# Moving the turned heads' scores and exponentials into the MLP stage of an attention-plus-MLP block

## The chip, the cores and the metric

The kernel runs on one core of a Trainium2 chip. The metric is the device time of one execution in microseconds (us). Before the change it is 1127.23 us, the median of three runs (1126.95 to 1127.47).

## The reference

The block adds attention and an MLP to its input. Both work on the normalised input; the MLP normalises it once more.

```python
def _A_ref(x, wq, wk, wv, wo):          # one k and v for all 16 heads
    q = (x @ wq).reshape(B, S, H, Dh).transpose(0, 2, 1, 3)
    k, v = x @ wk, x @ wv
    scores = einsum("bhqd,bkd->bhqk", q, k) * Dh ** -0.5
    o = einsum("bhqk,bkd->bhqd", softmax(scores), v)
    return o.transpose(0, 2, 1, 3).reshape(B, S, H * Dh) @ wo

def _B_ref(x, w1, b1, w2, b2):
    h = gelu(layernorm(x) @ w1 + b1)    # the tanh form of GELU
    return h @ w2 + b2

xn = layernorm(x)
return x + _A_ref(xn, ...) + _B_ref(xn, ...)
```

The sizes are S = 2048 tokens, D = 448, H = 16 heads of Dh = 28, F = 1792, all in float32. GELU in its tanh form is h(x) = x (0.5 + 0.5 tanh(0.79788 (x + 0.044715 x^3))).

## The kernel before

The tokens are cut into four row chunks of 512 (CT = 4 tiles of 128). Precision is kept by splitting float32 operands into a high and a low part (names ending in h and l) and adding the products. The order of all instructions is the order in which the Python code issues them: a manual schedule, each engine with its own queue in that order.

**First stage (to about 70 us).** x is loaded, normalised and transposed, q, k and v are projected, and q is stored to DRAM (`qd`). k stays in SBUF as `ks`, v as `vs`. All 16 row tiles of x stay in SBUF (`acc`), since the MLP result is later added to them. The second normalisation of chunk 0 is done here.

**MLP stage (70 to 485 us).** It is a row of 56 slots, 14 pieces of F for each of the four chunks. `slot(n)` issues the first product of piece n (`mlp1`, eleven 512-wide matmuls into the PSUM tile `ph`, of which there is one; the last is L174), then GELU on ACT straight from `ph` (L527), a copy to the high part `hh` (L530), the low part `hl` on POOL (L532), and then the second product of piece n-2 (`mlp2`, twelve 448-wide matmuls into four PSUM tiles `m2`, L541 to L545). Every matmul of these is a yield, and after 20 of each 46 yields (MLP_MAX) the loop issues one step of another job: the maxima. In slots 2, 3, 5, ... 13 of the first chunk the slot begins by splitting a part of w2 (ACT L321, then POOL L322, or DVE for the first one). During a chunk the next chunk is normalised and transposed (`norm_gen`): four times in a chunk four transposes (L254) go through the tile `ph`, issued after the sixth matmul of `mlp2` (`between`). b2 is added to a chunk's rows by POOL (L585).

**The maxima.** Softmax needs the maximum of each row of scores before the exponentials. Each head of each unit takes 16 matmuls of a q tile (`qm`, loaded from `qd`) with `ks` into one of three PSUM tiles `m` (L486), each followed by a DVE maximum (L487). Those that are not done in the MLP stage are done in the attention stage.

**Attention stage (485 to 1118 us).** There are 16 units: four row chunks by four groups of four heads. A unit takes eight steps of two key tiles. A step makes the transposed scores (keys on partitions) of the plain heads in pairs (`scores`, matmuls L795 into one of two PSUM tiles `s`, one exponential of 128x1024 on ACT for a pair, L797) and multiplies the previous step's exponentials with v (`pv`, L726, 16 matmul instructions a step in a block). The maxima enter those scores as two extra rows of the product.

**Turned heads.** In the units of TURNED (2 to 15) the fourth head goes another way. Its scores are made with queries on partitions (`turned_scores`, L746), so that DVE can scale them and find the maximum in one pass (L747, into `raw`), ACT takes the exponential with that maximum as bias (L764), 64 KB DMAs on the SP and POOL queues regroup them in SBUF (L768), and DVE transposes 32x32 blocks (L773). Such a unit has three plain heads: three pairs a step instead of four, and no separate maximum for the fourth head.

The order inside a step is written out in ORDERS, a string for units 0 and 1 each and one for the rest. p is a pair of scores with its exponential, m a maximum, t a turned score, x a turned exponential, T the block transposes, P the block of v products, n and o steps of the normalisation and of the output projection, e the load of the next unit's maxima. Maxima are issued only as far as a quota allows, which grows with `weight` from step to step; where it is used up, the m's that stand later in the string issue nothing. In the last 11 steps (LEAD) the weight is zero. The output projection (`o_jobs`, twelve 448-wide matmuls a row tile) lies in four steps after each chunk.

Of the kernel before, what the change touches and what calls it, by code (L numbers as in the profile page):

```python
# [15 lines left out]
P = 128  # L16
S, D, H, DH, F = 2048, 448, 16, 28, 1792
NT = S // P
CT = 4
# [17 lines left out]
def block_kernel(ctx, tc, x, wq, wk, wv, wo, w1, b1, w2, b2, out):  # L37
# [20 lines left out]
    ad = dram.tile([P, NT, D], F32, name="ad")  # L58
    qd = [dram.tile([D, S], F32, name=f"qd{i}") for i in range(2)]

    acc2 = keep.tile([P, CT, D], F32, name="acc2")
# [5 lines left out]
    acc1 = ph1.enter_context(tc.tile_pool(name="accp", bufs=1)).tile([P, NT - CT, D], F32, name="acc")  # L67

    def acc(t0, n=1):
        tile_, t0 = (acc1, t0) if t0 < NT - CT else (acc2, t0 - NT + CT)  # L70
        return tile_[:, t0:t0 + n, :]

    def row(t):
        return acc(t)[:, 0, :]

# [7 lines left out]
    b1t = wp.tile([P, NF], F32, name="b1t")  # L83
    b2b = wp.tile([P, D], F32, name="b2b")
# [4 lines left out]
    hrp = ph1.enter_context(tc.tile_pool(name="hrp", bufs=3))  # L89

    ph1a = ExitStack()
    wqp = ph1a.enter_context(tc.tile_pool(name="wqp", bufs=1))
    qpp = ph1a.enter_context(tc.tile_pool(name="qpp", bufs=4, space=PSUM))
# [6 lines left out]
    def load_x(t0, n):  # L100
        nc.sync.dma_start(acc(t0, n), xv[:, t0:t0 + n, :])
# [27 lines left out]
    qmt = [qmp.tile([P, CW], F32R, name=f"qm{i}") for i in range(3)]  # L129
    for t in qmt:  # L130
        pool.memset(f(t), 0.0)
# [63 lines left out]
    def bn(t):  # L195
        c = t // CT
        if t % CT == 0:
            sts[c] = tmp.tile([P, CT, 6], F32, name="st", bufs=2)
        dve.bn_stats(sts[c][:, t % CT, :], row(t))
# [20 lines left out]
    def norm_both():  # L220
# [8 lines left out]
        act.activation(warm, one, AF.Gelu_apprx_tanh)  # L229
        yield  # L230

    def norm_parts(c, second, first=False, bank=mtile):
# [5 lines left out]
        def center(k):  # L238
# [6 lines left out]
            act.activation(xn[:, 0:D], row(t), AF.Identity, bias=bias[:, t:t + 1], scale=scale[:, t:t + 1])  # L245
            dve.tensor_scalar(xn[:, D:512], row(t)[:, 384:448], scale[:, t:t + 1], bias[:, t:t + 1],
# [144 lines left out]
    def b1_turn():  # L391
        pb = mtile([P, NF])
        pe.transpose(pb, b1r, ident[0:NF, 0:NF])
        dve.tensor_copy(b1t, pb)

# [8 lines left out]
    def load_m(u, j, qm=None, q=None):  # L404
        c, g = units[u]
        if qm is None:
            qm = qmt[heads.index((u, j)) % 3]
# [8 lines left out]
    for c in range(NCH):  # L416
        center, turn = norm_parts((c + 1) % NCH, c + 1 == NCH)
        for i in range(4):
# [7 lines left out]
            if i in ((2, 3) if c == 0 else (1, 3)):  # L426
# [8 lines left out]
                if n in (2, 3):  # L435
                    qms.append(load_m(*heads[n - 2]))
            for job in more.get((c, i, True), ()):
# [38 lines left out]
    def max_stream():  # L476
        for h, (u, j) in enumerate(heads):
# [3 lines left out]
            for t in range(CT):  # L481
                for n in range(4):
                    if (t, n) == (0, 2) and h + 2 < len(heads):
                        qms.append(load_m(*heads[h + 2]))
# [26 lines left out]

    ph1b = ExitStack()
    hp = ph1b.enter_context(tc.tile_pool(name="hp", bufs=3))
# [7 lines left out]
    def mlp1(c, ft):  # L521
# [4 lines left out]
        hr = hrp.tile([P, CW], F32, name="hr", bufs=2)  # L526
        act.activation(hr, ph, AF.Gelu_apprx_tanh, bias=b1t[:, ft:ft + 1])  # L527
        hh = hrp.tile([P, CW], F32R, name="hh")
        hl = hrp.tile([P, CW], F32R, name="hl")
        act.activation(hh, hr, AF.Copy)  # L530
        hs[c, ft] = (hh, hl)
        pool.tensor_sub(hl, hr, f(hh))  # L532

    def mlp2(c, ft, between):
# [4 lines left out]
        for k in range(CT):  # L539
            ts = slice(k * P, (k + 1) * P)  # L540
            pe.matmul(m2[k], hh[:, ts], w2h[:, ft, :], start=(ft == 0), stop=False)  # L541
            yield
            pe.matmul(m2[k], hh[:, ts], w2l[:, ft, :], start=False, stop=False)  # L543
            yield
            pe.matmul(m2[k], hl[:, ts], w2h[:, ft, :], start=False, stop=(ft == NF - 1))  # L545
            if ft == NF - 1:
                a = row(CT * c + k)
                dve.tensor_add(a, a, m2[k])
                if k == CT - 1 and c < NCH - 1:
                    nc.sync.dma_start(ad[:, CT * c:CT * c + CT, :], acc(CT * c, CT))  # L550
            if k == 1:
                between()
# [329 lines left out]
```

## Time and profile before

| what | value |
|---|---|
| median of three runs | 1127.23 us |
| profiled execution, its own time | 1126.83 us |
| profiled execution, span | 1125.1 us |
| PE busy | 1110.3 us (99%) |
| weight loads (PEld) busy | 713.9 us (63%) |
| DVE busy | 898.1 us (80%) |
| ACT busy | 656.6 us (58%) |
| POOL busy | 474.3 us (42%) |
| DMA moved | 120.05 MB, mean 107 GB/s |

The busy times come from one profiled execution; the engines work side by side. PE is the matrix engine, ACT the activation engine, DVE the vector engine, POOL the general engine, SP the one that only issues DMAs. The durations of matmuls overlap, because they are pipelined, so the distance from one start to the next is what a matmul takes of PE's time. L with a number is a line of the code above. In rows of groups, the numbers behind the bar are busy us and mean ns of one, and behind the second bar the idle time before them with what ended it.

### The profile page before, as it was taken

Reading aid. Unit: us, or ns where it says so; the run is one execution under the profiler, and the core shown is the slowest. Engines: PE = TensorE matmul, PEld = TensorE weight load, DVE = VectorE, ACT = ScalarE, POOL = GpSimd, SP = SyncE. Lnnn points to the kernel's source line nnn. Section 1 sums busy time; section 2 is a strip of 40 time slices with the busy share of each in tenths; the row PEclk is TensorE's granted clock in tenths of the full one; section 3 lists DMA queues with packets and bytes.
Section 4 is the critical chain, followed back from the end, with each engine's and each line's share of the span. In section 5 each row is a group of like instructions: output and inputs, shape, how many; then the busy total and the mean of one; then the engine's idle time right before and its main releaser. Section 6 shows DMA issues by size and latency. Waiting matters only on the chain.

```text
span 1125.1 us, 17754 instructions
## 1 busy us (share of the span) xinstructions
PE 1110.3 (99%) x5793; PEld 713.9 (63%) x5793; DVE 898.1 (80%) x1676; ACT 656.6 (58%) x789; POOL 474.3 (42%) x719
## 2 busy tenths in 40 slices
PE   9999999999999999999999999999999999999998
PEld 8778888888888888854544445544446444455444
DVE  7789999999999999976677877677786777776743
ACT  6752221222222111256888888688886888886883
POOL 6332241113113112311566666366664666653640
PEclk9999999999999999999999999999999999999999
DMA  8661101000100012030455676455665556664520
GB/s 281 198 198 50 58 17 50 25 17 17 58 18 17 25 50 54 22 95 10 117 144 148 168 168 168 136 156 154 158 181 148 155 144 167 164 164 134 139 67 33
DMA packets 73928, 120.05 MB, mean 107 GB/s; under 512 B 24486, under 2 KB 34916, under 8 KB 73836
## 3 DMA queue, kind: packets, MB, share of 16 engines
q1 hardware_dynamic: 53228, 80.26, 25.2%
q0 software_dynamic: 19200, 38.08, 12.7%
q8 instruction: 46, 0.75, 0.3%
q10 hardware_dynamic: 1408, 0.57, 0.2%
q14 instruction: 46, 0.38, 0.1%
HBM read 45.19 MB, written 13.88 MB: 53 GB/s over the span
## 4 chain that ended last, share of the span: by engine, by line
PE 89%; DVE 6%; ACT 2%; issue 2%; DMA 1%; SPq 1%; POOL 0%; DVEq 0%; ACTq 0%; POOLq 0%
PE po L726 20%; PE s L795 18%; PE m L486 16%; PE ph L169 10%; PE m L746 4%; PE m L543 4%; PE m L545 4%; PE m L541 4%; DVE mx L487 3%; PE qp L169 2%; PE m L637 1%; ACT p L797 1%; PE ph L172 1%; PE ph L174 1%; PE m L639 1%
## 5 line engine op out<-in xcount | busy, mean ns | idle before, releaser
L487 DVE TENSOR_REDUCE mx<-m 128x1 f32<-128x512 f32 x800 | 525.9, 687 | 33.4 <-PE m L486 27.9
L797 ACT ACTIVATE p<-s 128x1024 f32<-128x1024 f32 x389 | 381.9, 1024 | 111.2 <-PE s L795 110.4
L486 PE MATMUL m<-ks,qm 128*128 128x512 f32 x800 | 319.9, 405 | 2.1 <-DVE raw L747 1.0
L795 PE MATMUL s<-xh,ks 128*128 128x512 f32 x778 | 261.2, 419 | 3.7 <-ACT p L797 1.8
L768 POOL DMA_DIRECT2D turned<-raw x336 | 168.1, 506 | 213.1 <-ACT raw L764 193.2
L747 DVE TENSOR_SCALAR_CACHE_REDUCE raw<-m 128x512 f32<-128x512 f32 x224 | 151.7, 684 | 119.4 <-PE m L746 95.2
L726 PE MATMUL po<-p,vs 128*32 128x512 f32 x2048 | 247.0, 598 | 0.0
L795 PEld LDWEIGHTS s<-xh,ks 128*128 128x128 f32 x778 | 131.1, 188 | 142.8 <-ACT p L797 109.0
L527 ACT ACTIVATE hr<-ph,b1t 128x512 f32<-128x512 f32 x56 | 38.5, 688 | 305.4 <-PE ph L174 281.6
L532 POOL TENSOR_TENSOR hl<-hr,hh 128x512 fp32r<-128x512 f32 x56 | 72.2, 1290 | 301.5 <-PE m L486 284.4
L486 PEld LDWEIGHTS m<-ks,qm 128*128 128x128 f32 x800 | 150.1, 188 | 54.5 <-DVE raw L747 21.0
L773 DVE STREAM_TRANSPOSE p<-turned 128x1024 f32<-128x1024 f32 x112 | 138.4, 1236 | 22.3 <-PE po L726 8.6
L726 PEld LDWEIGHTS po<-p,vs 128*32 128x32 f32 x2048 | 53.8, 109 | 121.5 <-issue 117.1
L764 ACT ACTIVATE raw<-raw,m 128x1024 f32<-128x1024 f32 x112 | 127.8, 1141 | 0.0
L746 PE MATMUL m<-ks,q 128*128 128x512 f32 x224 | 88.5, 395 | 0.0
L541 PE MATMUL m<-w2h,hh 128*128 128x448 f32 x224 | 82.4, 368 | 0.0
L545 PE MATMUL m<-w2h,hl 128*128 128x448 f32 x224 | 82.0, 366 | 0.0
L543 PE MATMUL m<-w2l,hh 128*128 128x448 f32 x224 | 81.9, 366 | 0.0
L169 PE MATMUL ph<-xh,w1l 128*128 128x512 f32 x168 | 66.2, 394 | 0.0
L169 PE MATMUL ph<-xl,w1h 128*128 128x512 f32 x168 | 66.1, 394 | 0.0
L169 PE MATMUL ph<-xh,w1h 128*128 128x512 f32 x168 | 66.0, 393 | 0.0
L746 PEld LDWEIGHTS m<-ks,q 128*128 128x128 f32 x224 | 42.1, 188 | 10.3 <-DVE raw L747 0.7
(151 smaller groups left out, 1100.1 us busy)
## 6 DMA issues: line engine op xcount, KB each, us to landing
turned<-raw SPq DMA_DIRECT2D x560, 64.0 KB
turned<-raw POOLq DMA_DIRECT2D x336, 64.0 KB, 2.3
xh<-qd POOLq DMA_DIRECT2D x56, 168.0 KB, 4.0
qm<-qd SPq DMA_DIRECT2D x160, 56.0 KB
qd<-qe SPq DMA_DIRECT2D x24, 256.0 KB
tr<-ld POOLq DMA_DIRECT2D x56, 64.0 KB, 2.6
raw<-in_B_w_dram SPq DMA_DIRECT2D x7, 448.0 KB
q<-qd SPq DMA_DIRECT2D x56, 56.0 KB
```

Of the source, the lines that this page charges most:

```text
L169: pe.matmul(ps, w, v, start=(n == 0), stop=False)
L486: pe.matmul(pm, qm[:, t * P:(t + 1) * P], ks[:, n * CW:(n + 1) * CW], start=True, stop=True)
L487: dve.tensor_reduce(mx[:, CT * j + t, n:n + 1], pm, axis=AX.X, op=ALU.max)
L541: pe.matmul(m2[k], hh[:, ts], w2h[:, ft, :], start=(ft == 0), stop=False)
L726: pe.matmul(po[32 * j:32 * j + 32, :], vs[:, kt, :], ps.pop((u, kt, j)), start=(kt == 0), stop=(kt == NT - 1))
L746: pe.matmul(sc, q3[i][:, t * P:(t + 1) * P], ks[:, n * CW:(n + 1) * CW], start=True, stop=True)
L747: dve.tensor_scalar(raw[:, :, 4 * n:4 * n + 4, :].rearrange("p r b i -> p b r i"), sc.rearrange("p (b r i) -> p b r i", r=4, i=32), SCALE, ...
L764: act.activation(raw[:, rs], raw[:, rs], AF.Exp, bias=m3[:, 4:5], scale=1.0)
L768: q.dma_start(turned[u][32 * r:32 * r + 32, 4 * t + a, :], raw[32 * a:32 * a + 32, r].rearrange("p b i -> p (b i)"))
L773: dve.transpose(p.rearrange("p k (g j) -> p g k j", j=32), turned[u][:, :, 32 * kt:32 * kt + 64].rearrange("p g (k j) -> p g k j", j=32))
L795: pe.matmul(s[:, i], ks[:, (kt + k) * P:(kt + k + 1) * P], qss[u][:, j, :], start=True, stop=True)
L797: act.activation(p, s, AF.Exp, scale=SCALE)
```

## The change

- Unit 1 is turned too: TURNED has 15 units.
- The turned heads are scored in the MLP stage. Of the steps that a slot issues beside its matmuls (18 of 46 yields now), the first four are turned scores (`tq.step()`), one row tile of a turned head per slot; the others are maxima. The last turned unit's 16 scores are left for the attention stage.
- The exponentials are taken in the MLP stage too, two of 128x1024 per slot, and stored to DRAM (`td`), four DMAs of 256 KB a row tile on SP. In the attention stage each half of a turned unit is read back by four DMAs of 512 KB, a unit ahead, in the order that the block transposes need. `raw` has two buffers instead of three.
- GELU is worked out from Tanh: Identity (`hx`) and Square (`hz`) read `ph` on ACT; POOL adds one and multiplies; ACT takes Tanh; POOL scales and multiplies; ACT copies the high part and POOL subtracts. The stages are issued at fixed places between the twelve `mlp2` matmuls of the slot: the norm's step after the second (before: the sixth), an exponential after the fourth and the seventh, Tanh after the fifth, the copy after the tenth.
- The rows of x are no longer kept: `line` reloads each row tile in the MLP stage, once for its second normalisation and once for the addition of the MLP result, which is then stored to `ad`. b2 is added row tile by row tile, in slots 11, 12 and 13 of a chunk and 0 of the next. The last chunk's rows are read back at the end like the others.
- The q tiles of the maxima have two buffers instead of three and are loaded one head ahead instead of two.
- ORDERS has one string for unit 0 and one for the others; `weight` is 4 a step in unit 0 and 5 afterwards.

The changed program issues 224 turned scores and 281 of 784 maxima in the MLP stage, and 503 maxima and 16 turned scores in the attention stage. Before, 560 of 800 maxima were in the MLP stage, and 240 maxima and all 224 turned scores in the attention stage.

```diff
-MLP_MAX = 20
-ORDERS = ("ptmpmmpmmenPptmmon", "ptpmmpmxenPptmonm", "ptmpTeonPpxtmn")
-TURNED = tuple(range(2, 16))
-RAWS = 3
+MLP_MAX = 18
+ORDERS = ("pmpmmpmmenPpmmonm", "ptmpmmeTnPpxmmon")
+TURNED = tuple(range(1, 16))
+RAWS = 2
+GELU = 0.044715, 0.7978845608028654
...
+    def line(t):
+        lines[t] = keep.tile([P, D], F32, name="a", bufs=4)
+        nc.sync.dma_start(lines[t], xv[:, t, :])
...
     def turned_exp():
...
         act.activation(raw[:, rs], raw[:, rs], AF.Exp, bias=m3[:, 4:5], scale=1.0)
-        for r in range(2 * h, 2 * h + 2):
-            for a in range(4):
-                q = pool if a == 3 or (a == 2 and r % 2) else nc.sync
-                q.dma_start(turned[u][32 * r:32 * r + 32, 4 * t + a, :],
-                            raw[32 * a:32 * a + 32, r].rearrange("p b i -> p (b i)"))
+        if h == 1:
+            for a in range(4):
+                nc.sync.dma_start(td[u][:, :, 4 * t + a, :],
+                                  raw[32 * a:32 * a + 32].rearrange("p r (h b) i -> p (r h) (b i)", h=2))
+            stored[u] = t
...
     def mlp1(c, ft):
...
-        hr = hrp.tile([P, CW], F32, name="hr", bufs=2)
-        act.activation(hr, ph, AF.Gelu_apprx_tanh, bias=b1t[:, ft:ft + 1])
-        hh = hrp.tile([P, CW], F32R, name="hh")
-        hl = hrp.tile([P, CW], F32R, name="hl")
-        act.activation(hh, hr, AF.Copy)
-        hs[c, ft] = (hh, hl)
-        pool.tensor_sub(hl, hr, f(hh))
+        hx = hrp.tile([P, CW], F32, name="hx", bufs=2)
+        hz = hrp.tile([P, CW], F32, name="hz", bufs=2)
+        act.activation(hx, ph, AF.Identity, bias=b1t[:, ft:ft + 1])
+        act.activation(hz, ph, AF.Square, bias=b1s[:, ft:ft + 1], scale=GELU[0] ** 0.5)
+        pool.tensor_scalar(hz, hz, 1.0, 1.0, op0=ALU.mult, op1=ALU.add)
+        pool.tensor_mul(hz, hz, hx)
+
+        def middle():
+            act.activation(hz, hz, AF.Tanh, scale=GELU[1])
+            pool.tensor_scalar(hz, hz, 0.5, 0.5, op0=ALU.mult, op1=ALU.add)
+            pool.tensor_mul(hx, hx, hz)
+
+        def ending():
+            hh = hrp.tile([P, CW], F32R, name="hh")
+            hl = hrp.tile([P, CW], F32R, name="hl")
+            act.activation(hh, hx, AF.Copy)
+            hs[c, ft] = (hh, hl)
+            pool.tensor_sub(hl, hx, f(hh))
...
     def slot(n):
...
+        stages = {1: norms.get(n, none), 3: turned_exp, 4: middle, 6: turned_exp, 9: ending}
...
+        ts = 0
         for _ in slot(n):
             done += 1
             if n < len(mslots) + 1 and done * MLP_MAX // 46 > (done - 1) * MLP_MAX // 46:
-                maxed += mxs.step()
-        if (c, ft) == (NCH - 1, NF - 1):
-            act.activation(warm, one, AF.Exp)
+                if ts < 4 and n < len(mslots):
+                    ts += tq.step()
+                else:
+                    maxed += mxs.step()
...
+    def load_d(u, h):
+        halves[u, h] = att.tile([P, 4 * CT, 256], F32, name="half", bufs=3)
+        for r in range(4):
+            nc.sync.dma_start(halves[u, h][32 * r:32 * r + 32], td[u][:, 2 * r + h, :, :])
...
-    weight = [0 if n >= len(steps) - LEAD else 24 if n < 6 else 16 if u < 2 else 6 for n, (u, kt) in enumerate(steps)]
+    weight = [0 if n >= len(steps) - LEAD else 4 if u == 0 else 5 for n, (u, kt) in enumerate(steps)]
...
+        if kt % 8 == 0 and u + 1 < NU:
+            load_d(u + 1, kt // 8)
```

More of the change, by code (lines that the diff above doesn't have):

```diff
@@ L394, in b1_turn @@
         dve.tensor_copy(b1t, pb)
+        pool.tensor_scalar(b1s, b1t, GELU[0] ** 0.5, 0.0, op0=ALU.mult, op1=ALU.add)
     later(3, 0, b1_turn)
@@ L546, in mlp2 @@
             if ft == NF - 1:
-                a = row(CT * c + k)
+                t = CT * c + k
+                a = lines.pop(t)
                 dve.tensor_add(a, a, m2[k])
[L549 to L552, printed above, removed]
+                nc.sync.dma_start(ad[:, t, :], a)
+            stages[3 * k + 2]()
             yield
```

157 lines of the change are left out of this document (81 added, 76 removed).

## The prediction

> **What bounds the kernel now.** I read the chain of waits first, then busy time by stage, then the timeline of one MLP slot and of one attention step. The chain that ended last, by engine:
>
> ```profile
> PE 89%; DVE 6%; ACT 2%; issue 2%; DMA 1%; SPq 1%; POOL 0%; DVEq 0%; ACTq 0%; POOLq 0%
> ```
>
> The PE queue sets the time. Stages (start and end, length, then busy us and count of PE, PEld, DVE, ACT, POOL): two pieces of the MLP's first row chunk, from one slot's last projection matmul (L174) to another's; its chunks 2 to 4; attention unit 0; unit 1; the 101 steps with a turned head that still place maxima; one plain MLP slot; one slot with transposes; four attention steps with the output projection.
>
> ```profile
> 69.56:80.01 10.45, 9.66 (x38) 6.71 (x37) 10.32 (x17) 3.48 (x5) 2.59 (x2) 1.00 0.29 73
> 80.01:169.80 89.79, 89.79 (x413) 75.60 (x412) 83.91 (x132) 25.90 (x38) 32.60 (x22) 1.00 0.15 46
> 169.80:475.47 305.67, 305.46 (x1387) 255.86 (x1386) 285.22 (x448) 64.40 (x99) 67.92 (x54) 1.00 0.11 32
> 493.54:536.37 42.83, 41.12 (x215) 20.20 (x214) 28.68 (x54) 28.19 (x34) 5.41 (x5) 1.00 0.20 49
> 536.37:581.42 45.05, 44.57 (x240) 22.35 (x239) 31.11 (x71) 39.54 (x43) 24.72 (x46) 1.00 0.43 123
> 581.42:1067.32 485.90, 483.60 (x2740) 237.06 (x2740) 367.06 (x759) 401.21 (x429) 291.38 (x522) 1.00 0.59 157
> 304.69:311.98 7.29, 7.29 (x34) 6.19 (x33) 7.01 (x13) 1.97 (x3) 1.29 (x1) 1.00 0.12 34
> 319.28:327.13 7.85, 7.85 (x39) 6.50 (x37) 7.52 (x13) 2.57 (x4) 1.29 (x1) 1.00 0.00 1
> 689.77:717.57 27.80, 27.77 (x152) 17.24 (x152) 18.10 (x37) 17.94 (x20) 12.63 (x24) 1.00 0.56 149
> ```
>
> A plain slot is 33 matmuls in 7.29 us (the 34th reaches in), with ACT busy 1.97 and POOL 1.29: reserve on both. In the attention steps ACT is busy 401 of 486 us. The granted clock is 1.00 throughout.
>
> **MLP: what a slot becomes.** PE in a plain slot, starts and durations:
>
> ```profile
> 304.69 0.39 PE L174 MATMUL ph<-xl,w1h 128*128 128x512 f32 x1
> 304.92 0.39 PE L486 MATMUL m<-ks,qm 128*128 128x512 f32 x1
> 305.15 0.36 PE L541 MATMUL m<-w2h,hh 128*128 128x448 f32 x1
> 305.35 0.37 PE L543 MATMUL m<-w2l,hh 128*128 128x448 f32 x1
> ```
>
> Starts lie 0.23 us apart after a 512-wide matmul, 0.20 after a 448-wide one. MLP_MAX 18 instead of 20 gives nine score steps per slot for ten: 7.06 us, over 56 slots **-12.9**.
>
> Four of the nine are turned scores, with two exponentials per slot on ACT, and GELU is now Identity, Square, two POOL operations, Tanh, two POOL operations, Copy, and POOL's subtraction as before. ACT in a slot, then POOL behind it:
>
> ```profile
> 305.18 0.69 ACT L527 ACTIVATE hr<-ph,b1t 128x512 f32<-128x512 f32 x1 [5.94 <-PE ph L174]
> 305.90 0.63 ACT L530 ACTIVATE hh<-hr 128x512 fp32r<-128x512 f32 x1
> 306.44 0.75 ACT L245 ACTIVATE xn<-acc,lnqb,lnq 128x448 f32<-128x448 f32 x1
> ```
> ```profile
> 306.67 1.29 POOL L532 TENSOR_TENSOR hl<-hr,hh 128x512 fp32r<-128x512 f32 x1 [6.00 <-PE m L486]
> ```
>
> ACT follows PE by 0.10 us (304.69+0.39 to 305.18), POOL follows ACT by 0.14 (306.53 to 306.67), and independent activations overlap by 0.09 (306.44). POOL in the attention stage:
>
> ```profile
> 614.98 1.31 POOL L678 TENSOR_TENSOR oc<-oc,tr 128x512 f32<-128x512 f32 x1
> 616.39 0.61 POOL L684 TENSOR_SCALAR oth<-oc 128x512 fp32r<-128x512 f32 x1
> 617.09 1.29 POOL L685 TENSOR_TENSOR otl<-oc,oth 128x512 fp32r<-128x512 f32 x1
> ```
>
> So a multiply takes 1.31, a scalar operation 0.61, with 0.1 between. Square and Tanh are not in the trace; I take 0.69 and 0.64, from L527 and L530. ACT runs its queue in order, so the next slot's Identity stands behind this slot's Copy. The loop: Identity 0.69-0.09, Square 0.69, 0.14, POOL 0.61+0.10+1.31, 0.10, Tanh 0.64, 0.14, POOL 2.02, 0.10, Copy 0.63-0.09 = **6.99 us against a slot of 7.06**. Plain slots stay on PE's pace, but with no reserve: what is put into the loop is paid.
>
> Transposes of the next chunk (12 slots) use the bank `ph`. They moved from after the sixth MLP-2 matmul to after the second, and `ph` is now free only after Square. PE is there 0.23+0.20+0.23+0.20 = 0.86 after L174 starts; Square ends at 0.39+0.10+0.60+0.69 = 1.78. Wait 0.97 with latency, and 0.10 for the slower restart (rows in the attention part): 12 x 1.07 = **+12.9** (0 if the loop were early, 23 if it runs 0.9 late).
>
> ```profile
> L585 POOL TENSOR_TENSOR acc<-acc,b2b 128x448 f32<-128x448 f32 x16 | 17.9, 1152 | 0.0
> L322 POOL TENSOR_TENSOR w2l<-raw,w2h 128x896 fp32r<-128x896 f32 x6 | 12.7, 2122 | 4.3 <-ACT w2h L321 4.1
> ```
>
> The six splits of w2 in chunk 1 stand on POOL ahead of a slot's first GELU operation, which had no room to give: 6 x 2.1 = 12.6. Four slots there are transpose slots of 7.06+(7.85-7.29)+1.07 = 8.7 us, in which the loop (about 7.4 with the norm's ACT work) gains 1.3 each: **+7.4** net (0 to 12.6). The adds of b2 stand in the same place four slots a chunk, mostly drained before the next wait: **+2**.
>
> The first split is worse: ACT's copy of w2h and DVE's subtraction stand at the start of slot 2 behind the Copy of slot 1.
>
> ```profile
> L321 ACT ACTIVATE w2h<-raw 128x896 fp32r<-128x896 f32 x7 | 6.6, 942 | 0.0
> ```
> ```profile
> L322 DVE TENSOR_TENSOR w2l<-raw,w2h 128x896 fp32r<-128x896 f32 x1 | 1.4, 1447 | 0.0
> ```
>
> Two loops after slot 0's L174, 0.49+2x7.0 = 14.5, then 0.94 and 1.45: DVE is held until 16.9, and slot 2's turned scores behind it; with three PSUM banks the fourth waits, and slot 2 ends near 17.9 instead of 10.45: **+7.4** (5 to 8). At the other end hl of the last slot comes 8.7 us after L174 where 7.6 would do: **+2** (0 to 4). MLP together -12.9+12.9+7.4+2+7.4+2 = **+18.8**.
>
> What is queued behind the new waits: the stores of exponentials (60 row tiles, four DMAs each, on SP) wait for the second exponential; behind them stand the loads of q rows (issued 14 maxima ahead, nearly three slots) and of x rows (two slots ahead), so nothing comes late. The tile `raw` has two buffers: its first writer two slots later comes 11.6 us after L174; the second exponential ends near 5.7, the fourth store is issued near 7.5, so it may take 4.2 us.
>
> ```profile
> xh<-qd POOLq DMA_DIRECT2D x56, 168.0 KB, 4.0
> ```
>
> That is the nearest landing (168 KB for 256). It just fits; I cost it at nothing. [...]
>
> **Attention: what a step becomes.** PE in a step, and ACT:
>
> ```profile
> 623.75 0.74 PE L795 MATMUL s<-xh,ks 128*128 128x512 f32 x2
> 624.33 0.40 PE L746 MATMUL m<-ks,q 128*128 128x512 f32 x1
> 624.56 0.63 PE L795 MATMUL s<-xh,ks 128*128 128x512 f32 x2
> 625.03 0.39 PE L746 MATMUL m<-ks,q 128*128 128x512 f32 x1
> 625.26 0.39 PE L486 MATMUL m<-ks,qm 128*128 128x512 f32 x1
> 625.67 0.73 PE L795 MATMUL s<-xh,ks 128*128 128x512 f32 x2
> 626.33 1.92 PE L726 MATMUL po<-p,vs 128*32 128x512 f32 x16
> 628.18 0.73 PE L795 MATMUL s<-xh,ks 128*128 128x512 f32 x2
> ```
> ```profile
> 624.59 1.03 ACT L797 ACTIVATE p<-s 128x1024 f32<-128x1024 f32 x1 [0.62 <-PE s L795]
> ```
> ```profile
> 515.81 0.73 PE L795 MATMUL s<-xh,ks 128*128 128x512 f32 x2 [0.24 <-ACT p L797]
> ```
>
> Three pairs of scores C, A, B share two tiles `s`, so B waits for the exponential of C: 624.59+1.03 = 625.62, and B starts at 625.67, 1.92 after C; in the earlier step that wait is named. (A pair after a pause takes 0.58 to 0.66, one in flow 0.47.) Before, the two or three other matmuls all lie between C and B, where that wait covers them. A step is 1.92 + 0.66 + the po block 1.85 = 4.43.
>
> After, 503 of 784 maxima are left for attention (240 of 800 before): 4.4 a step (503 over 577 units of weight, five a step). The order "ptmpmmeTnPpxmmon" fills them in from its front: one after A, two after B, and what is left, 1.4, after C. C 0.58, 1.4 x 0.23, A 0.47, 0.23: B could start at 1.60 and still waits until 1.92. **The two behind B have no cover: 4.43+0.46 = 4.89.** That ACT lost the 112 exponentials here is no help, for B needs only C's, which ACT begins at once either way.
>
> Per part: the 12 steps with the output projection cost 27.80/4 = 6.95; there its twelve matmuls come to lie between C and A and cover the wait: 0.58+0.3+12x0.2+0.47+0.23+0.47+0.46+0.1+1.85 = 6.86, -1. The other 89 average (485.90-12x6.95)/89 = 4.52, to 4.89: +32.9. Unit 1 drops from four pairs to three, 45.05/8 = 5.63 to 4.89: -5.9. Unit 0 (7 steps, 6.12) takes 3.5 maxima (weight 4): B at 1.92, two maxima, D at 2.96, then 0.66+0.1+1.85 = 5.57: -3.9. The last 11 steps hold no maxima before or after; some turned work ahead goes: -1. **Attention +21** (bounds: 0, if B were early; +40, if also DVE delays the maxima).
>
> ```profile
> L773 DVE STREAM_TRANSPOSE p<-turned 128x1024 f32<-128x1024 f32 x102 | 126.0, 1236 | 6.7 <-DMA turned<-raw 2.9 <-DMA q<-qd 2.0 <-DMA qm<-qd 1.9
> L487 DVE TENSOR_REDUCE mx<-m 128x1 f32<-128x512 f32 x159 | 108.9, 685 | 0.0
> ```
>
> DVE's step is 4.4x0.685+1.24 = 4.25 of 4.89: it keeps up. The read back (512 KB a DMA, eight steps or 39 us ahead) and POOL's DMA issues that go cost and gain nothing; POOL is nowhere on the chain. The table load dropped at the MLP's end lay beside ten us of matmuls: nothing.
>
> **Sum.** The profiled execution took 1126.83 (span 1125.1), 0.4 under the median of 1127.23. 1126.8+18.8+21 = **1167**.
>
> **Rivals.** (1) The ACT-POOL loop is shorter than worked out and PE never waits in the MLP: 1126.8-12.9+21 = 1135. For it: the reserve before; against: the sum of rows is 6.99. (2) B's wait is no floor and the added maxima fill gaps: attention 0, so 1146. PEld is busy 237 of 486 us there, PE 484. [...] The 0.24 us wait on ACT speaks against it: the room is a wait that comes too early in the step to be filled from behind B. (3) Faster: PE is bound by its number of matmuls alone and waits no more than before. 16 fewer (-16 maxima, +16 turned, -16 scores) x 0.23 = -3.7: 1123. It decides if Square frees `ph` before 0.86 us and C's exponential ends within 1.6 us of C; the rows say 1.78 and 1.9. (4) Slower still: the loop outgrows the slot. [...] (5) It doesn't do what it says: its instruction order has the 224 turned scores in the MLP and no table loads between Tanh and Exp, so hardly.
>
> **Chances.** Forecast 0.56 (own range 1152 to 1184), (1) 0.10, (2) 0.10, (3) 0.07, (4) 0.15, no difference 0.02. Range 1135 to 1205: from (1) to the middle of (4). A measurement here can tell about 0.2%: faster 0.07, within it 0.02, slower 0.91.
>
> **What would show it.** Slots 7.06 where plain and 8.5 or more with transposes, PE's idle before them named as ACT's `hz`; slot 2 near 13 us after slot 1; in attention B 1.92 after C, then two maxima, then po, steps of 4.9. Wrong it is if slots run over 7.3 throughout, if `raw`'s writers wait for a DMA, or if steps come near 4.5.

## The result, and the profile after

The changed kernel took 1178.2 us (median of four runs, 1178.14 to 1179.59) beside 1127.3 for the kernel before on the same chip: 1.0455 times as long, interval 1.0437 to 1.0473. The forecast was 1167, its own range 1152 to 1184. The profiled execution has a span of 1177.7 us, 52.6 more than that of before.

The chain of waits by engine, to be held against PE 89% before:

```profile
PE 68%; POOL 11%; ACT 10%; issue 4%; DVE 3%; DMA 2%; SPq 1%; ACTq 0%; POOLq 0%; DVEq 0%
```

POOL and ACT, which held 0% and 2% of the chain, now hold a fifth of it. POOL's part is for the most part GELU's loop; of ACT's 10%, 6% are the exponentials of attention (L830), which held 1% before. Busy time by stage, in the columns of the prediction's table (window, length, busy us and count of PE, PEld, DVE, ACT, POOL, then granted clock, DMA share, GB/s). The rows are: MLP slots 1 and 2; slots 3 to 14; the rest of the MLP; attention unit 0; unit 1; the 101 steps with maxima; a plain slot; a slot with transposes; four steps with the output projection.

```profile
71.27:93.48 22.21, 11.88 (x39) 8.23 (x38) 10.90 (x26) 9.94 (x13) 10.11 (x10) 0.88 0.52 125
93.48:193.75 100.27, 92.58 (x402) 77.03 (x400) 82.04 (x180) 64.60 (x86) 77.16 (x70) 0.94 0.69 176
193.75:501.42 307.67, 296.56 (x1346) 248.02 (x1345) 258.72 (x606) 197.84 (x262) 221.99 (x216) 1.00 0.73 183
521.13:560.74 39.61, 35.73 (x193) 16.30 (x193) 16.38 (x29) 28.18 (x34) 6.06 (x6) 1.00 0.89 195
560.74:600.77 40.03, 39.10 (x217) 18.59 (x216) 34.62 (x55) 25.01 (x28) 14.16 (x23) 1.00 0.41 94
600.77:1121.14 520.37, 506.36 (x2829) 253.51 (x2828) 422.02 (x612) 308.02 (x336) 176.06 (x288) 1.00 0.71 160
298.83:305.86 7.03, 7.03 (x33) 6.01 (x32) 6.06 (x15) 3.98 (x5) 6.08 (x6) 1.00 0.64 161
259.29:267.78 8.49, 7.71 (x38) 6.33 (x37) 7.04 (x18) 5.97 (x9) 6.16 (x6) 1.00 0.76 183
720.03:747.49 27.46, 27.46 (x155) 18.14 (x154) 18.65 (x28) 13.31 (x16) 9.00 (x17) 1.00 0.71 183
```

The MLP, from the first slot's last projection matmul to the last one's, takes 430.15 us for 405.91 (+24.2); attention from the first po block to the last 644.2 for 619.2 (+25). The other 3.4 lie before the MLP (1.7), where PE waits that much for a load of q, and between MLP and attention (1.6). In the 101 steps ACT is busy 308 us for 401: the change did take that work from ACT, and these steps grew by 34.5 all the same. The granted clock (the last column but two) has changed too: it was 1.00 everywhere and is 0.88 and 0.94 in the first two rows.

An attention step, PE and then ACT (three exponentials in one row):

```profile
948.94 0.73 PE L828 MATMUL s<-xh,ks 128*128 128x512 f32 x2
949.52 0.62 PE L491 MATMUL m<-ks,qm 128*128 128x512 f32 x2
949.98 0.62 PE L828 MATMUL s<-xh,ks 128*128 128x512 f32 x2
950.43 0.39 PE L491 MATMUL m<-ks,qm 128*128 128x512 f32 x1
950.86 0.74 PE L828 MATMUL s<-xh,ks 128*128 128x512 f32 x2
951.43 0.63 PE L491 MATMUL m<-ks,qm 128*128 128x512 f32 x2
```
```profile
949.77 2.88 ACT L830 ACTIVATE p<-s 128x1024 f32<-128x1024 f32 x3 [1.97 <-PE s L828]
```

C starts at 948.94, B at 950.86, 1.92 later, with three maxima before it and two behind it, and then the po block at 951.99: the step as forecast. In the MLP, a slot with transposes:

```profile
245.56 0.66 PE L256 MATMUL ph<-ident,xn 128*128 128x128 f32 x4 [0.78 <-ACT hz L572]
```

PE stands for 0.78 us until Square (L572) has read `ph`. Three things were not forecast. In slot 1 ACT waits 8.88 us before it may write `hx`, and PE behind it:

```profile
76.01 0.69 ACT L571 ACTIVATE hx<-ph,b1t 128x512 f32<-128x512 f32 x1 [8.88 <-DMA qd<-qe]
...
77.32 0.50 PE L164 MATMUL ph<-xh,w1h 128*128 128x512 f32 x1 [4.15 <-ACT hz L572]
```

`hx` now lies in memory of the stage before, and waits until the last transfer out of `qe` there has ended. In slot 2 the forecast wait of PE comes, and what follows it is slow:

```profile
92.46 0.80 PE L525 MATMUL m<-ks,q 128*128 128x512 f32 x1 [5.42 <-DVE raw L526]
93.05 0.63 PE L167 MATMUL ph<-xh,w1h 128*128 128x512 f32 x1
93.48 0.63 PE L169 MATMUL ph<-xl,w1h 128*128 128x512 f32 x1
```

Starts of 512-wide matmuls lie 0.43 us apart here and until 98.2, and 0.23 after. And the writers of `raw` wait for the stores of exponentials (us in total, times, longest), three times in chunk 1 (4.1 us), twice in chunk 3 (1.1) and six times in chunk 4 (6.5):

```profile
DVE raw L526 <- DMA td<-raw: 11.7, 11, 2.2
```

### The profile page after: what moved, and what is told of

Same layout as the page of the kernel before. It is cut to its first block, busy times and chain, and to the rows that moved or that the text cites. A ratio compares the mean times of both kernels' runs of the same rounds, so it can differ in the third digit from the quotient of the medians.

```text
span 1177.7 us, 16968 instructions
## 1 busy us (share of the span) xinstructions
PE 1116.2 (95%) x5777; PEld 715.9 (61%) x5777; DVE 914.3 (78%) x1704; ACT 726.4 (62%) x899; POOL 558.3 (47%) x679
## 4 chain that ended last, share of the span: by engine, by line
PE 68%; POOL 11%; ACT 10%; issue 4%; DVE 3%; DMA 2%; SPq 1%; ACTq 0%; POOLq 0%; DVEq 0%
PE po L796 20%; PE s L828 16%; PE m L491 10%; ACT p L830 6%; PE ph L164 5%; POOL hz L574 3%; POOL hx L579 3%; PE m L525 3%; PE m L603 2%; PE m L597 2%; PE m L600 2%; POOL hl L586 2%; PE qp L164 2%; DMA td<-raw 1%; ACT hz L577 1%
## 5 line engine op out<-in xcount | busy, mean ns | idle before, releaser
L492 DVE TENSOR_REDUCE mx<-m 128x1 f32<-128x512 f32 x784 | 511.0, 686 | 115.9 <-PE m L491 107.8
L830 ACT ACTIVATE p<-s 128x1024 f32<-128x1024 f32 x381 | 367.8, 1024 | 234.8 <-PE s L828 234.1
L491 PE MATMUL m<-ks,qm 128*128 128x512 f32 x784 | 287.5, 398 | 1.7 <-DVE mx L492 0.8
L810 DVE STREAM_TRANSPOSE p<-half 128x1024 f32<-128x1024 f32 x120 | 147.8, 1232 | 5.9 <-PE po L796 5.9
L543 ACT ACTIVATE raw<-raw,m 128x1024 f32<-128x1024 f32 x120 | 137.1, 1142 | 0.0
L525 PE MATMUL m<-ks,q 128*128 128x512 f32 x240 | 96.0, 400 | 12.5 <-DVE raw L526 9.1
L586 POOL TENSOR_TENSOR hl<-hx,hh 128x512 fp32r<-128x512 f32 x56 | 72.2, 1290 | 41.6 <-ACT hh L584 40.8
L744 POOL DMA_DIRECT2D tr<-ld x56 | 28.2, 508 | 113.4 <-DMA ld<-rc 113.4
L412 POOL DMA_DIRECT2D qm<-qd x112 | 57.4, 519 | 40.7 <-PE m L491 32.1
L574 POOL TENSOR_TENSOR hz<-hz,hx 128x512 f32<-128x512 f32 x56 | 72.5, 1294 | 4.7
L579 POOL TENSOR_TENSOR hx<-hx,hz 128x512 f32<-128x512 f32 x56 | 72.3, 1291 | 4.7
L577 ACT ACTIVATE hz<-hz 128x512 f32<-128x512 f32 x56 | 35.3, 631 | 61.4 <-POOL hz L574 61.4
L584 ACT ACTIVATE hh<-hx 128x512 fp32r<-128x512 f32 x56 | 35.4, 632 | 60.3 <-POOL hx L579 60.3
```

What stands on the lines that cost most here:

```text
L491: pe.matmul(pm, qm[:, t * P:(t + 1) * P], ks[:, n * CW:(n + 1) * CW], start=True, stop=True)
L492: dve.tensor_reduce(mx[:, CT * j + t, n:n + 1], pm, axis=AX.X, op=ALU.max)
L525: pe.matmul(sc, q3[i][:, t * P:(t + 1) * P], ks[:, n * CW:(n + 1) * CW], start=True, stop=True)
L543: act.activation(raw[:, rs], raw[:, rs], AF.Exp, bias=m3[:, 4:5], scale=1.0)
L574: pool.tensor_mul(hz, hz, hx)
L579: pool.tensor_mul(hx, hx, hz)
```

## The experiments

**The maxima moved from behind B to behind C (x1).** Two of the forecast's steps are at issue: that B waits and that the maxima behind it have no cover.

```diff
-ORDERS = (..., "ptmpmmeTnPpxmmon")
+ORDERS = (..., "ptmmpeTnPpxmmmon")
```

> The changed kernel with one string of ORDERS changed: the maxima of a turned step stand two behind C and two behind A instead of one behind A and two behind B, so that they lie between C and B; nothing else moves. Theory 1 (B may not start before C's exponential ends, 1.92 us after C, and what stands behind B is uncovered): the step goes from 4.89 to C 0.58 + four maxima 0.92 to 1.0 + A 0.47 = 2.0, + 0.66 + 1.85 = 4.55; over 97 steps that is -31 us, so 1147 against 1178. Rival (a step costs what its matmuls cost, wherever the maxima stand): no change, 1178. Rival (DVE sets the step, 4.25 us of work in it): the maxima behind each other wait for DVE and the step stays above 4.75, 1165 or more.

Measured 1171.5, ratio 1.0386 (1.0369 to 1.0403): 6.7 us gained of the 31 expected. Steps without the output projection average 4.80 for 4.92. By the number of maxima in them: in the changed kernel the 43 steps with four and the 25 with five, and no other matmul beside scores and products, all take 4.89, so the fifth costs nothing there; here those with four take 4.49 and those with five 5.10. One with five:

```profile
946.15 0.73 PE L828 MATMUL s<-xh,ks 128*128 128x512 f32 x2
...
947.90 1.10 PE L491 MATMUL m<-ks,qm 128*128 128x512 f32 x2
948.84 0.63 PE L828 MATMUL s<-xh,ks 128*128 128x512 f32 x2
```

B (948.84) now comes 2.69 after C, so it no longer waits for C's exponential; but five maxima stand close, and the last of them waits for one of the three banks that DVE must empty (its start lies 0.60 behind that at 947.90, instead of 0.23; over the run the weight loads of these matmuls wait 48.1 us for DVE's maxima, 3.1 in the changed kernel). So theory 1 holds where four maxima are placed (4.49, for the 4.55 worked out), and with five DVE holds the step longer than the wait had done: the rival named for this run, which gave 1165 or more.

**Half an exponential each (x2).** The exponential of a pair was cut into two, in the same tile, so that B's first matmul could start earlier.

```diff
-        act.activation(p, s, AF.Exp, scale=SCALE)
+            act.activation(p[:, i], s[:, i], AF.Exp, scale=SCALE)   # behind each matmul
```

> The changed kernel with the exponential of a pair of scores taken in two halves of 512 columns, each as soon as its matmul is done; the order of the matmuls is as in the changed kernel. Theory 1: the first half of C is through 0.44 + 0.10 + 0.60 = 1.14 us after C starts, the second near 1.7, so B starts when the queue gets there, 1.6 us after C, instead of 1.92: steps of 4.57 to 4.65 instead of 4.89, -25 to -30 us, 1148 to 1153. Rival (a step costs what its matmuls cost): no change, 1178. Rival (ACT becomes the bound: six halves of 0.60 and 0.04 between are 3.9 us of a step): no loss expected below 4.4 us a step.

Measured 1708 and 1746 us in two runs, far from any expectation. One row of the list of waits (us in total, times, longest), and the attention steps as a window:

```profile
PE s L828 <- ACT p L830: 294.1, 380, 1.7
```
```profile
560.00:1200.00 640.00, 479.66 (x1865) 185.75 (x1865) 283.99 (x418) 256.05 (x441) 119.44 (x192) 0.79 0.37 85
```

The second matmul of a pair waits until the exponential of the first half has read the tile: in this run the order is kept by tile, not by half. So each pair pays matmul, exponential, matmul in turn, and with these waits all through the stage, 0.77 us on average and 1.7 at the longest, the granted clock is 0.79 there, for 1.00 in the changed kernel's steps. The run tells nothing of the floor; x5 makes the same test with separate tiles.

**Square reads `hx` (x3).** It frees `ph` one operation earlier.

```diff
-        act.activation(hz, ph, AF.Square, bias=b1s[:, ft:ft + 1], scale=GELU[0] ** 0.5)
+        act.activation(hz, hx, AF.Square, scale=GELU[0] ** 0.5)
```

> The changed kernel with Square reading hx from SBUF instead of ph, so that ph is free after Identity. Theory 2 (the twelve transpose slots wait for ph until Square ends): the wait of 0.78 us plus restart shrinks by 0.5 to 0.6 in each, -7 us, 1171; transpose slots of the later chunks go from 8.50 to 7.95. Rival (what paces these slots is the loop over ACT and POOL, not ph): Square now starts after Identity ends, the loop grows by 0.1, and nothing is won: 1178 to 1183.

Measured 1178.2 (two runs), ratio 1.045 (1.0429 to 1.047): no change in the whole. In the slots there is one:

```profile
243.68 0.36 PE L600 MATMUL m<-w2l,hh 128*128 128x448 f32 x1
...
244.19 0.33 PE L256 MATMUL ph<-ident,xn 128*128 128x128 f32 x1
```

PE's gap before the transposes is 0.15 us for 0.78, the slots take 8.03 for 8.50, and the MLP 425.3 for 430.2. The profiled run lost those 4.8 elsewhere: 1.8 before the MLP, 1.2 behind it, 1.1 in attention. So the wait for Square is real, and taking it away is worth about half a us a slot; a gain of 3 or 4 us in the total is within what two runs leave open.

**Memory of their own for `hx` and `hz` (x4).** They leave the pool that takes over the first stage's memory; `mr` gets 9 buffers for 14 and `hz` one for two to make room.

```diff
-        hx = hrp.tile([P, CW], F32, name="hx", bufs=2)
+        hx = hxp.tile([P, CW], F32, name="hx", bufs=2)      # pool opened ahead of the first stage
```

> The changed kernel with hx and hz (hz with one buffer) in memory of their own, not in that of the first stage's pool; nothing else moves but the number of buffers of the small maxima tiles. Theory 3 (the 4.2 us stall in slot 1 is Identity of slot 0 waiting for the last store of q, whose memory hx reuses, and the half clock after it is a consequence of the stall): the stall goes, slot 1 takes near 6 instead of 10.98 us, PE's starts stay 0.23 apart there, and of the 4.2 + 1.9 some 4 to 6 us stay won: 1172 to 1174. Rival (the fill of the chain sets the first slots, so the wait only moves to slot 2): 1178, slot 2 longer by what slot 1 loses.

Measured 1175.8, ratio 1.0428 (1.0407 to 1.0449). Slots 1 to 3, in the changed kernel, here, and in x8 (below), each in a row (the second row of x8 is one of its slots with transposes):

```profile
71.27:102.66 31.39, 21.06 (x70) 15.95 (x69) 17.35 (x42) 15.39 (x20) 15.56 (x16) 0.84 0.49 120
```
```profile
72.72:98.72 26.00, 19.57 (x71) 14.55 (x69) 17.03 (x42) 15.17 (x20) 14.46 (x15) 0.87 0.55 135
```
```profile
71.12:93.71 22.59, 19.60 (x70) 14.39 (x69) 15.90 (x40) 14.38 (x19) 14.33 (x14) 0.85 0.54 148
252.37:263.98 11.61, 9.52 (x38) 7.41 (x36) 8.36 (x19) 5.66 (x8) 6.33 (x6) 0.85 0.79 195
```

5.4 us go from these slots, and ACT's wait for `qe` is gone from the list of waits; the MLP takes 424.2. The first of the unforeseen things is shown in the slots; the 2.4 us by which the total is shorter are within what the two intervals leave open.

**Score tiles of one bank (x5).** Four tiles of one bank in place of two of two, with an exponential each.

```diff
-    sp = ctx.enter_context(tc.tile_pool(name="sp", bufs=2, space=PSUM))
+    sp = ctx.enter_context(tc.tile_pool(name="sp", bufs=4, space=PSUM))
...
-        s = sp.tile([P, 2, CW], F32, name="s")
         for i, (k, j) in enumerate(jobs):
-            pe.matmul(s[:, i], ...)
+            s = sp.tile([P, CW], F32, name="s")
+            pe.matmul(s, ...)
+            act.activation(p[:, i], s, AF.Exp, scale=SCALE)
-        act.activation(p, s, AF.Exp, scale=SCALE)
```

> The six score matmuls of an attention step go to four tiles of one bank each instead of two tiles of two banks, and each has its own exponential (0.60 us, six a step, 3.6 us of ACT instead of 3.1). Theory 1 (the step's floor is the wait of the pair B for C's two-bank exponential, 1.92 us after C): a single bank is free about 1.1 us after C starts, so B no longer waits and the step is PE's own work, 1.85 for the po block, 6 x 0.233 for scores, 4.4 x 0.233 for maxima and 0.3 of restarts, about 4.55 instead of 4.89: 105 steps x 0.34 = -36, about 1142 us. Rival (DVE, the three banks of the maxima, paces the steps, as the run with the reordered maxima left 4.76): steps 4.75, about 1162. Rival (the step is bound by its matmuls and not by the wait): 1178.

Measured 1151.9, ratio 1.0222 (1.0205 to 1.0239): 26 us less than the changed kernel.

```profile
860.77 0.74 PE L828 MATMUL s<-xh,ks 128*128 128x512 f32 x2
...
862.28 0.67 PE L828 MATMUL s<-xh,ks 128*128 128x512 f32 x2
...
863.33 1.93 PE L796 MATMUL po<-p,vs 128*32 128x512 f32 x16
```
```profile
861.31 3.05 ACT L829 ACTIVATE p<-s 128x512 f32<-128x512 f32 x6 [1.37 <-PE s L828]
```

B starts 1.51 after C and waits for nothing; the next C comes 4.42 after this one, and the mean of those without the output projection is 4.65 for 4.92, or 4.60 without the two steps around 994 us, where PE waits 2.59 us for a load of `qm`. The same matmuls in the same order, so the floor was the wait for C's exponential. Of the ten us missing to 1142, some four are those two steps and four to five the 4.60 for the 4.55 worked out; the others were not followed. Six small exponentials cost ACT 3.05 us where three large ones cost 2.88, not 3.6.

**The po block in two halves (x6, and x7 on the kernel before).** Half a block now stands behind C, so that B is covered without touching ACT.

```diff
+            elif what == "h":
+                if n:
+                    pv(*pvq.pop(0))
...
-"ptmpmmeTnPpxmmon"
+"pmptmeTnhpxmhmmon"     # x7: "ptmpTeonPpxtmn" -> "pmptTenhpxtmhon"
```

> The block of po matmuls is cut in two halves, one behind C and one behind B, and the maxima are spread singly over the step (A, m, B, m, turn, half block, C, m, half block, m, m). Theory 1 (B waits for C's exponential): half a block 0.95 us and A 0.47 now lie between C and B, so B does not wait; two more restarts cost 0.2: steps about 4.65 instead of 4.89, 97 steps x 0.24 = -23, about 1155 us. Rival (DVE and the banks of the maxima): spread singly they do not queue, so if this was what held the run with the reordered maxima at 4.76, this run shows no wait of a maximum for its bank. Rival (no floor; steps are bound by matmul work): 0.2 more a step, about 1198.

> The kernel before with its block of po matmuls cut in two halves, one behind C and one behind B. Theory 1 (the same wait of B for C's exponential set its step of 4.52): PE's own work there is about 4.0 + 0.2 of restarts = 4.2, ACT's is 3 x 1.03 + 1.14 + 0.1 = 4.3, so steps of about 4.35: 89 x 0.17 = -15, about 1112 us. Rival (the kernel before was bound by its matmuls): 0.2 a step more, about 1147. Rival (ACT, with a turned exponential between the exponentials of C and A, already sets the pace): no change, 1127.

Measured 1177.9 (ratio 1.0448, 1.0433 to 1.0464) and 1139.2 (ratio 1.0105, 1.009 to 1.012). The 101 steps of the first and of the second:

```profile
599.87:1116.95 517.08, 516.15 (x2829) 242.38 (x2828) 425.85 (x614) 314.50 (x335) 175.36 (x288) 1.00 0.71 161
```
```profile
581.72:1077.91 496.19, 496.19 (x2741) 225.95 (x2740) 378.18 (x757) 407.46 (x430) 291.20 (x523) 1.00 0.56 153
```

PE is busy 516 of 517 and 496 of 496 us: no wait is left in either, as the theory has it, and yet nothing is gained. Cutting the block was priced at 0.2 a step and costs about 0.3: the first half's last matmul is followed after 0.52 instead of 0.41, the matmul ahead of the second half takes 0.33 and the first behind it 0.34, instead of 0.23. Steps come to 4.83 and 4.62. The wait went, the price of the cut took its place: in the changed kernel the 101 steps are 3.3 us shorter, and the last eleven, which hold no maxima to cover, 3.4 longer.

**Three parts of the MLP (x8).** `hx` and `hz` as in x4, the first split of w2 given out at the end of slot 0, and the transposes behind the sixth MLP-2 matmul.

```diff
-        if n == 2 or (2 < n < NF and n % 2 == 1):
+        if 2 < n < NF and n % 2 == 1:                 # split(0) at the end of slot 0
...
-        stages = {1: norms.get(n, none), 3: turned_exp, 4: middle, 6: turned_exp, 9: ending}
+        stages = {3: turned_exp, 4: middle, 5: norms.get(n, none), 6: turned_exp, 9: ending}
```

> Three changes of the MLP stage alone: hx and hz in memory that no earlier stage holds (as in the run before, 1175.8), the first split of w2 given out at the end of slot 0 instead of the start of slot 2, and the transposes of the next chunk behind the sixth MLP-2 matmul instead of the second. Theory (the terms of the prediction): slot 2 loses its wait of 5.4 us and the slow matmuls after it, -6; the twelve slots with transposes lose the wait for Square, 8.50 to about 7.85, 12 x 0.65 = -8: about 1162 us. Rival (the loop over ACT and POOL is what these slots wait for, as the run with Square reading hx suggested): transposes that come later put ACT's norm work later into the loop, slots stay at 8.0 to 8.5, and only slot 2 gains: about 1169.

Measured 1209.9, ratio 1.0735 (1.0717 to 1.0753), 34 us slower than x4. The split did what it should: slots 1 to 3 take 22.59 for 26.00. The transposes did the opposite: their slots take 10.1 to 15.5 us (the second row of x8's windows above). One of them:

```profile
256.24 0.63 ACT L579 ACTIVATE hz<-hz 128x512 f32<-128x512 f32 x1 [1.08 <-POOL hz L576]
...
258.04 0.69 DVE L260 TENSOR_TENSOR xl<-ph,xh 128x512 fp32r<-128x512 f32 x1 [1.78 <-ACT xh L259]
...
258.78 0.50 PE L166 MATMUL ph<-xh,w1h 128*128 128x512 f32 x1 [1.99 <-DVE xl L260]
```

ACT's copy out of `ph` now stands behind Tanh, which waits for POOL; DVE's subtraction reads `ph` after it, and the next slot's projection, which writes that bank, waits for both. Neither theory had this. The early place of the transposes costs 0.8 us a slot, and a late one several.

**The new GELU alone (x9).** The kernel before with only GELU's nine operations and the early transposes; turned scores and exponentials stay in attention. (One `hz` buffer; q rows in two buffers for three, to make room.)

```diff
-        act.activation(hr, ph, AF.Gelu_apprx_tanh, bias=b1t[:, ft:ft + 1])
+        act.activation(hx, ph, AF.Identity, bias=b1t[:, ft:ft + 1])
+        act.activation(hz, ph, AF.Square, ...)      # and POOL, Tanh, POOL as in the change
```

> The kernel before with the new GELU alone (Identity, Square, two POOL operations, Tanh, two POOL operations, Copy; one hz buffer; transposes behind the second MLP-2 matmul as in the change; q rows in two buffers, loaded one head ahead, to make room). Turned scores, their exponentials and the number of maxima stay as before. Theory 1 (the prediction's terms lie in GELU's loop, and the exponentials only fill pauses of ACT): twelve waits for Square +12, w2's splits and b2's adds on POOL +8, slot 2 +5 to 7: about 1153 us. Rival (the turned exponentials on ACT and their scores on DVE make those waits): only the wait for Square is left, about 1139. In both the attention stage keeps its 619 us.

Measured 1162.2, ratio 1.031 (1.0295 to 1.0326). Slots 1 and 2, a slot with transposes, the whole MLP:

```profile
70.12:88.43 18.31, 10.55 (x38) 7.20 (x37) 11.11 (x18) 5.78 (x9) 10.09 (x10) 0.88 0.15 47
...
230.04:238.95 8.91, 8.14 (x38) 6.42 (x37) 7.11 (x13) 3.78 (x6) 6.40 (x6) 1.00 0.00 1
70.12:506.44 436.32, 413.86 (x1836) 339.23 (x1835) 375.83 (x595) 157.18 (x250) 308.62 (x295) 0.99 0.11 34
```

The MLP takes 436.3 for 405.9. Slots 1 and 2 hold 18.31 for 10.45, +7.9; twelve slots with transposes 1.04 each over the 7.87 of before, +12.5; 4.3 in one slot come from the two q buffers of this run (PE waits 2.46 us for a load of qm there) and are not the GELU's. Without those 4.3 the MLP is 26.1 us longer with GELU alone. The changed kernel's is 24.2 longer although each of its 55 slots saves 0.26, 14.3 in all, so it pays 38.5: two thirds of that come with GELU, without one exponential. That is theory 1 in the main, but not in all its terms. The splits of w2 cost 0.9 here and not 7.4: but for one, the slots with transposes in chunk 1 are as long as later ones. In the changed kernel slots are 0.3 shorter and ACT has the exponentials to take as well; which of the two makes the splits dearer there was not tested. Between MLP and attention lie 7.5 us more than before, where 2 were forecast and the changed kernel has 1.6: here the four adds of b2 stand in a row on POOL ahead of the last GELU operations, 4.42 us of the chain from 500.41 on.

**Single-bank tiles in the kernel before (x10).** The edit of x5.

> The kernel before with single-bank score tiles and six exponentials a step. Theory 1 (two limits lie close together there: the wait of B for C's exponential, 1.92 us, and ACT, whose step is 3 x 1.03 + 1.14 for a turned exponential + 0.1 = 4.3): taking the wait away raises ACT to 6 x 0.60 + 1.14 + 0.1 = 4.8 a step, so ACT paces: 89 x 0.3 = +27, about 1154 us. Rival (only the wait of B holds the step): 89 x -0.25 = -22, about 1105. The same edit gave the changed kernel 26 us, since its ACT had no turned exponentials left in this stage.

Measured 1111.1 (four runs, 1110.37 to 1111.46), ratio 0.9853 (0.9837 to 0.987): 1.5% less than the kernel before. Theory 1 of this run falls, its rival stands. The 101 steps, then ACT in one:

```profile
577.58:1051.29 473.71, 472.07 (x2740) 238.81 (x2740) 365.83 (x756) 416.68 (x731) 290.62 (x522) 1.00 0.60 161
```
```profile
641.36 1.09 ACT L796 ACTIVATE p<-s 128x512 f32<-128x512 f32 x2 [0.51 <-PE s L795]
...
643.37 2.71 ACT L796 ACTIVATE p<-s 128x512 f32<-128x512 f32 x5
```

I had put six exponentials at 0.60 end to end. Two take 1.09 and five 2.71, as each begins before the last has ended: some 0.53 each. ACT rises from 401 to 417 us of the stage only, does not pace it, and steps fall from 4.51 to 4.39.

Set beside it, the same steps of x5 tell what the wait was worth to the change:

```profile
594.62:1090.78 496.16, 492.63 (x2828) 256.66 (x2828) 420.27 (x613) 322.93 (x639) 175.38 (x288) 1.00 0.75 168
```

With the wait in neither kernel these steps still grow by 22.5 us, some four of them in the two steps around 994, for 34.5 with it in both. So more than half of their growth is the work itself, 88 matmuls more at some 0.23 us, and the rest, 12 to 16 us, comes of the wait, which covered more of the matmuls before the change than after it.

**The changed kernel repaired (x11).** x3, x4, x5 and the first split of x8 together.

> The changed kernel with single-bank score tiles (1151.9 by itself), hx and hz in memory of their own (-2.4 by itself), the first split of w2 at the end of slot 0 (slots 1 to 4 gave 3.4 in the run of three parts) and Square reading hx (transpose slots 0.5 shorter, -4). If the parts add up: about 1142 us; if the slots give back what Square and the bank gain to the loop over ACT and POOL: 1146. The kernel before, 1127, would be reached only if the loop's excess in chunks 1 and 4 went too, which none of these parts touches.

Measured 1142.7, ratio 1.0135 (1.012 to 1.015), as the sum of the parts gave. Its MLP:

```profile
71.75:491.89 420.14, 401.95 (x1784) 327.75 (x1782) 348.06 (x810) 274.27 (x361) 309.13 (x295) 1.00 0.71 182
```

PE does 402 us of work in an MLP of 420, and the slots with transposes, chunk 1 and chunk 4 hold the rest. It stays behind the kernel before, and 32 us behind the kernel before with the same tiles.

## Why the prediction was right

The direction, the place and the mechanism held; the size was 11 us short. By its steps:

- **Plain slots**: 7.03 for 7.06. **The loop** that was to leave no reserve is shorter than the 6.99 worked out:

```profile
252.74 0.69 ACT L571 ACTIVATE hx<-ph,b1t 128x512 f32<-128x512 f32 x1 [1.57 <-PE ph L169]
...
258.88 0.63 ACT L584 ACTIVATE hh<-hx 128x512 fp32r<-128x512 f32 x1 [1.07 <-POOL hx L579]
259.78 0.69 ACT L571 ACTIVATE hx<-ph,b1t 128x512 f32<-128x512 f32 x1 [0.27 <-PE ph L169]
```

Identity to the end of the Copy is 6.77, and ACT still waits 0.27 for PE. Rival (4), the loop outgrowing the slot, has no support in plain slots. Its size, and with it the range's upper end of 1205, was the author's estimate, and no run shows it: in the changed kernel POOL's multiplies for GELU take 1.26 to 1.31 us and its scalar operations 0.62 to 0.65, where the loop was summed from 1.31 and 0.61.
- **Transposes**: 0.90 us a slot for 1.07 (8.50 against 7.03 + 0.56); twelve times 1.07 is 12.8, not 12.9. Rival (1), no wait in the MLP, falls.
- **w2's splits**: slots 6, 8, 10, 12 and 14 are over their kind by 1.3, 0.8, 0.4, 0.4 and 4.1, together 7.0 for the 7.4 of the forecast. That agreement is in part luck. More than half of it is slot 14, where an add of b2 on POOL and the copy of w2h on ACT make Square late, PE pauses 2.27 us, and 512-wide matmuls then start 0.43 us apart instead of 0.23 for some 6 us (granted clock 0.60 from 184 to 192); and x9, with the same splits, loses 0.9 to them.
- **b2's adds**: nothing of the +2 is seen in chunks 2 and 3. The slots behind the adds (26 to 29 and 40 to 43) have the length of their kind.
- **Slot 2**: the wait came (5.42 us at the place named). x9, with nothing of the turned heads, has +7.9 in slots 1 and 2 for the 7.4. The changed kernel has 22.21 for 10.45, +11.8, and 2.2 more in slot 3. What the term lacked is the wait of `hx` for old memory (x4: -5.4 over three slots) and the lower clock behind each long wait (granted 0.66 from 77 to 82 us and 0.56 from 92 to 99). This is the largest miss of the sum.
- **Stores, costed at nothing**: a step that failed. 4.2 us were to cover the landing of the fourth store, issued 1.8 us behind the exponential. SP takes 3.3 us to issue the four, and in chunk 4 they also stand behind stores of `a` and loads of q:

```profile
421.11 2.62 SPq L608 DMA_DIRECT2D ad<-a  x2
...
425.60 3.33 SPq L546 DMA_DIRECT2D td<-raw  x4
```
```profile
427.69 5.39 DMA td<-raw
```

The second row is from the chain: from the issue of the fourth store here to its landing are 5.39 us, and 5.38 and 4.84 at the two other places where the chain names it (306.83 and 472.01). The 4.0 us that the prediction took from the loads of `xh` (168 KB, issued on POOL) is 0.8 to 1.4 shorter than these stores took. PE waits for a writer of `raw` in slots 13, 18, 30, 45, 46, 50 and 52, which are over by 5.7 us together. In four of them the trace names the store; in 18, 45 and 50 it names a matmul, but the one that the writer reads had ended 1.6 to 2.3 us before, so the store is left. The prediction's own sign of error ("if `raw`'s writers wait for a DMA") showed. It is read from the trace; no run took it away.
- **The first unit's maxima**, not in the sum: slot 53 is over by 2.0. ACT copies these maxima (`mn`) only behind GELU's Copy, which waits for POOL, and DVE and PE wait behind it. x9, which stores no exponentials in the MLP, has the same wait (1.55):

```profile
485.48 0.25 ACT L476 ACTIVATE mn<-m 16x128 fp32r<-16x128 f32 x1
```
```profile
486.09 0.50 PE L525 MATMUL m<-ks,q 128*128 128x512 f32 x1 [1.59 <-DVE mn L477]
```

- **Attention**: +25 for +21. Steps without the output projection 4.92 for 4.89; with it 27.46/4 = 6.87 for 6.86; unit 0 -3.2 for -3.9, unit 1 -5.0 for -5.9. That ACT's lost work would not help was right: x5 shows that the stage waited for the latency of one exponential, while ACT was idle 40% of the time.
- **Rival (2)**, that B's wait is no floor, falls with x5: in the changed kernel PEld is busy 253.5 of 520 us and PE 506, and the time came down, by 26 us, only when the tiles were changed, not because the added maxima found room. **Rival (3)**, PE bound by its count of matmuls, is what the attention steps of x10 and x6 come near to once their waits are gone.

The 52.6 us of the spans: 24.2 in the MLP where 16.8 were forecast, 3.4 at its two ends for 2, and 25 in attention for 21.

## What to carry to other kernels

A wait that covers work is a resource: before moving matmuls, find which of them lie under a wait and which do not, for here the same matmul costs nothing in one place (steps of four and of five maxima both take 4.89 in the changed kernel) and its full 0.23 us in another. A busy share (ACT's 308 of 520 us) did not show a floor made of one latency; giving the waiting pair tiles of its own took it away in both kernels (26 and 16 us), where moving work around it only put another limit in its place. And the longer chain over two engines cost here not its busy time but every place that shared a buffer or a queue with the short one.

## What the runs showed of the hardware that was not expected

Behind some pauses PE ran at about half rate for some us. In the changed kernel the starts of 512-wide matmuls lie 0.43 us apart, instead of 0.23, for some 4 to 6 us behind pauses of 4.15, 5.42 and 2.27 us, and the granted clock of slots 1 and 2 is 0.88. Single pauses of 1.73, 1.53 and 1.59 us (at 68.90, 134.61 and 486.09) left the rate alone there, and so did a pair of 1.40 and 0.68 us at 510. Of the pauses near 2 us in x8 some were followed by the half rate and some were not: 1.99 us at 258.78 by 0.43, 1.98 us at 393.48 and 2.11 us at 314.37 by 0.23. In x2, where PE's waits for the exponentials are 0.77 us on average and 1.7 at the longest, the granted clock is 0.79 over 640 us.

Breaking the flow of PE between full matmuls and the 32-column po matmuls cost about 0.3 us each time by the starts in x6, and 0.23 by the mean steps (4.83 against the 4.60 of x5, 4.62 against the 4.39 of x10), so here a block is dearer in two halves. And six one-bank exponentials behind one another take ACT 3.05 us against 2.88 for three of two banks: in flow the smaller size cost 6%, not the 16% that 0.60 against 1.03 suggests.
